# Keys of 14 tiles summed by transfers from GpSimd in place of additions on VectorE, in a linear-attention block with an MLP

## The chip, the cores and the metric

One Trainium2 chip; the kernel uses one core of it. The metric is the device time of one execution in microseconds (us). A core has TensorE (PE, matmuls and, on a track of its own, PEld, the loads of its weights), VectorE (DVE), ScalarE (ACT), GpSimd (POOL) and SyncE (SP), which here only issues transfers (DMAs). Each engine runs its own list of instructions in order; engines wait for one another through semaphores. Transfers are carried out by 16 DMA engines that all issuers share.

## The reference

The input is one sequence of 2048 rows with 512 features. The kernel computes a linear-attention block with 32 heads and then a two-layer MLP, both with a layer norm ahead and a residual behind:

```
h  = x + A(layernorm(x), wqkv, wo)
h2 = h + relu(layernorm(h) @ w1) @ w2            # 512 -> 1792 -> 512

A:  q, k, v = split((x @ wqkv)), 32 heads of 16
    phi(t) = where(t > 0, t + 1, exp(t)) + 1e-6
    pq, pk = phi(q), phi(k)
    kv  = sum over s of pk[s] (outer) v[s]       # per head, 16 x 16
    z   = sum over s of pk[s]                    # per head, 16
    o   = (pq @ kv) / (pq . z + 1e-6)
    A   = o @ wo
```

The change concerns z, the sum of the key features pk over all 2048 rows.

## The kernel before

**Tiling.** The 2048 rows are 16 tiles of 128 rows (`t` = 0 to 15), each tile with its rows on the 128 partitions. Transposed data (features on partitions) is kept in 4 chunks of 512 rows. All intermediate data stays on the chip.

**Order.** There is no automatic scheduling. The string `ORDER` (line 18 on) lists all work as words such as `K.5.1`; the name picks a function `op_...`, the numbers are its arguments. The words are issued in this order, and each engine runs its own part of the list in that order. So a word that waits holds up all later words of the same engine, and no others directly.

**Words around the change**, in the order in which a key tile passes through them:

- `S`, `A` (VectorE): statistics of a tile of x; `R` (ScalarE): 1/sqrt of the variance; `N` (VectorE, line 251): the normalized tile.
- `T` and `E` or `V`: transpose of the normalized tile on TensorE and its copy by ScalarE or VectorE; for most tiles `X` (line 291) instead, a transposing transfer issued by SyncE.
- `K` (TensorE, line 299): the keys of one tile, four matmuls into one PSUM bank.
- `F` (ScalarE, line 317): exp of the keys; `U` (ScalarE, line 320): relu of the keys; `M` (VectorE, line 324): min(exp, 1) + 1e-6; `D` (VectorE, line 327): their sum, pk, in bf16. From tile 4 on these four words handle two tiles at once.
- `G` (TensorE, line 351): adds the tile's part of x-transposed times pk into four banks, from which kv is later made.
- `za` (VectorE, line 358): adds two tiles of pk to `z_acc`, an fp32 array of 128 partitions by 2 x 512, one half for the even tile and one for the odd tile of each pair. It lies in memory that the MLP uses only later. `za.2` adds the pairs (0, 1) and (2, 3); five more words add one pair each, up to tiles 12 and 13.
- `zf` (VectorE, lines 362 to 364): adds the two halves of `z_acc` and splits the fp32 result into two bf16 arrays, value and remainder.
- `z` (TensorE, line 370): column sums over the 128 partitions: for each of the four blocks of 128 features, four matmuls of one column each, over pk of tiles 14 and 15 and the two arrays of `zf`.
- `zc`, `zh` (VectorE): z out of PSUM and, masked by head, as the matrix that the denominators (`dn`, TensorE, line 448) multiply.

Between these stand `Q` (TensorE, line 307), the queries, with `qF`, `qU`, `qM`, `qD` for their features, and words that load weights through SyncE: `lk`, `lq`, `lv`, `lo`, `l1`, `l2`. GpSimd builds masks at the start and has no other work.

`ORDER` has the following stretch on VectorE around the end of the sums (words of other engines left out): `M.10.2 za.8 D.12.2 D.10.2 za.10 za.12 ... M.14.2 ... zf.12 D.14.2 ... qM.0.0.2 qD.0.2.2 zc qD.0.0.2 zh`. On TensorE it is `K.14.2 G.9 K.15.3 G.10 Q.0.3.1 Q.0.2.0 G.11 G.12 z.0.2.14 z.2.2.14 z.1.2.14 z.3.2.14 G.13 G.14 dn.0.0 G.15`.

Of the kernel before, what the change touches and what calls it, by code (L numbers as in the profile page):

```python
# [9 lines left out]
ALU = mybir.AluOpType  # L10
# [6 lines left out]

ORDER = """
const table lx.0.1 lx.2.1 S.0 lx.1.1 S.2 A.0 S.1 A.2 R.0.1 N.0 R.2.1 lx.3.1 lk.0.2 lx.4.2 masks warm.1.7
warm.9.7 A.1 R.1.1 T.0.6 S.3 warm.1.7 N.2 T.2.4 N.1 A.3 E.0 R.3.1 T.1.5 lk.2.2 S.4 E.1 N.3 A.4 V.2 S.5 A.5  # L20
K.0.6 lx.6.2 K.1.3 T.3.1 F.0.1 U.0.1 lx.8.4 E.3 K.2.0 M.0.1 S.6 D.0.1 K.3.2 A.6 S.7 F.1.1 M.1.1 lx.12.4 R.4.2
N.5 A.7 N.4 U.1.1 D.1.1 F.2.1 U.2.1 R.6.2 S.8 S.9 N.7 A.9 A.8 M.2.1 N.6 lq.0.2 G.0 T.5.1 E.5 T.4.3 G.1 X.7
K.5.1 D.2.1 E.4 K.4.0 R.8.2 T.6.3 G.2 N.9 X.9 F.3.1 U.3.1 S.12 N.8 S.13 X.8 lq.2.2 M.3.1 A.13 A.12 D.3.1 E.6
K.6.2 F.4.2 R.12.2 U.4.2 K.7.3 G.3 M.4.2 S.11 F.6.2 U.6.2 N.12 D.4.2 S.10 S.14 N.13 M.6.2 A.11 A.10 D.6.2 A.14
R.10.2 X.12 K.9.1 G.4 N.11 S.15 N.10 A.15 X.13 K.8.0 G.5 G.6 za.2 U.8.2 F.8.2 X.11 X.10 G.7 R.14.2 K.13.1
K.12.0 M.8.2 N.15 D.8.2 za.4 N.14 K.11.3 K.10.2 G.8 l2.0.3 F.12.2 U.12.2 za.6 X.15 X.14 Q.0.0.0 F.10.2 Q.0.1.1
lv.2.2 l1.0.2 M.12.2 lv.0.2 l2.10.4 U.10.2 qU.0.0.2 qF.0.0.2 M.10.2 za.8 D.12.2 D.10.2 za.10 za.12 K.14.2 G.9
K.15.3 F.14.2 U.14.2 G.10 Q.0.3.1 Q.0.2.0 M.14.2 qF.0.2.2 qU.0.2.2 G.11 zf.12 D.14.2 G.12 z.0.2.14 z.2.2.14
z.1.2.14 z.3.2.14 qM.0.2.2 l2.7.3 lo.0.2 lo.2.2 l1.2.2 qM.0.0.2 qD.0.2.2 G.13 zc G.14 qD.0.0.2 zh dn.0.0 G.15
gD.2.2 gD.0.2 Q.1.1.3 Q.1.0.2 dnl.0 dnx.0.0.2 Q.1.2.0 dnx.0.2.2 kv.3.4 kv.0.4 kv.1.4 kv.2.4 Q.1.3.1 qF.1.0.2  # L30
qM.1.0.2 kx qF.1.2.2 qW.1.0.2 dt.0 dt.3 dt.2 dt.1 m.2.6 m.1.5 m.3.7 m.0.4 mA.0.2 Q.2.0.2 Q.2.1.3 qM.1.2.2
mA.2.2 qW.1.2.2 dn.1.5 dm.0.0.2 dm.0.2.2 dnl.1 dnx.1.2.2 Q.2.3.1 h.3.5 hD.3 h.0.6 h.1.7 hD.0 s.3 dnx.1.0.2
dt.6 Q.2.2.0 dt.4 dt.7 dt.5 qF.2.0.2 qU.2.0.2 h.2.6 hD.1 Q.3.0.2 Q.3.1.3 s.0 qF.2.2.2 qU.2.2.2 s.1 qU.3.0.2
a.3 a.0 hD.2 qM.2.0.2 n.0 a.1 n.1 dm.1.0.2 dm.1.2.2 n.3 s.2 Q.3.2.0 Q.3.3.1 qD.2.0.2 a.2 qM.2.2.2 n.2 qF.3.0.2
qF.3.2.2 l2.3.4 x.0 qM.3.2.2 qD.2.2.2 h.5.6 h.7.7 h.6.5 x.1 t.2.3 r.0.4 e.2 h.4.4 x.3 dn.2.3 dnl.2 dnx.2.0.2
p.0.0.2 dt.8 hD.6 qM.3.0.2 qW.3.2.2 hD.4 p.0.1.3 qD.3.0.2 hD.5 dnx.2.2.2 pA.0.0.2 p.0.3.1 p.0.2.0 dn.3.6
pD.0.2.2 p.0.5.3 p.0.4.2 pD.0.4.2 p.0.7.1 p.0.6.0 p.0.13.3 s.6 dt.10 p.0.12.2 dt.11 dt.9 hD.7 a.6 s.5 dm.2.0.2
dm.2.2.2 dnl.3 pA.0.6.2 a.5 pD.0.12.2 f.2.6.0.7 s.7 h.11.7 h.9.0 p.0.9.3 h.8.5 p.0.8.2 dnx.3.2.2 dnx.3.0.2
hD.9 a.7 hD.11 p.0.10.0 f.3.7.0.7 p.0.11.1 h.10.4 dt.15 pA.0.10.2 pD.0.8.2 dt.14 dt.13 dt.12 s.4 s.9 n.5
dm.3.2.2 s.11 hD.8 a.11 dm.3.0.2 hD.10 n.7 f.2.6.7.7 h.13.5 h.15.4 n.6 hD.15 a.4 n.4 s.8 h.14.1 f.3.7.7.7  # L40
h.12.2 f.0.4.0.7 x.5 x.6 s.10 hD.14 a.10 hD.13 hD.12 n.10 x.4 s.13 s.12 x.7 n.11 a.9 a.8 f.1.5.0.7 a.12 s.15
p.1.1.1 p.1.0.0 pA.1.0.2 f.1.5.7.7 a.15 s.14 fo.2 p.1.8.0 p.1.9.1 n.12 a.13 fo.3 n.15 n.13 fo.1 pD.1.8.2
f.0.4.7.7 a.14 n.8 p.1.12.0 p.1.13.1 p.1.2.2 p.1.3.3 p.1.10.6 r.12.4 r.4.4 pA.1.12.2 n.9 x.11 x.15 x.10 x.9
x.8 pD.1.2.2 p.1.7.5 p.1.5.1 fd.2 fd.3 p.1.4.0 p.2.3.3 p.2.2.2 n.14 fo.0 pD.1.4.2 pD.2.2.2 fd.0 x.13 x.14
p.2.0.0 p.1.11.7 p.2.7.3 p.2.1.1 r.8.4 pA.2.0.2 p.2.6.2 p.1.6.4 pD.2.6.2 p.2.4.0 pA.1.10.2 pA.1.6.2 p.2.5.1
pA.2.4.2 f.7.7.0.7 p.2.12.0 p.2.13.1 f.4.4.0.7 f.5.5.0.7 p.2.10.2 f.4.4.7.7 p.2.11.3 f.6.6.0.7 pD.2.10.2
pD.2.12.2 fd.1 x.12 f.6.6.7.7 f.5.5.7.7 p.2.8.0 p.2.9.1 p.3.2.2 p.3.3.3 fo.6 pD.2.8.2 fo.4 fo.5 p.3.4.0
f.7.7.7.7 p.3.5.1 pA.3.4.2 pD.3.2.2 fo.7 f.10.6.0.7 p.3.1.1 f.9.5.0.7 p.3.7.3 p.3.0.0 f.8.4.0.7 p.3.6.2 fd.6
f.9.5.7.7 f.11.7.0.7 f.10.6.7.7 fd.4 fd.5 fd.7 pA.3.0.2 pA.3.6.2 f.8.4.7.7 p.3.12.0 fo.9 f.11.7.7.7 p.3.13.1
p.3.11.3 p.3.10.2 pD.3.10.2 fo.8 fo.11 pA.3.12.2 p.3.9.1 f.13.5.0.7 p.3.8.0 f.12.4.0.7 pA.3.8.2 fo.10 fd.10  # L50
fd.9 f.13.5.7.7 f.14.6.0.7 fo.13 f.12.4.7.7 f.15.5.0.14.3.1 f.14.6.7.7 f.15.7.0.14.0.2 fd.13 fd.8 fd.11 fo.12
fo.14 fo.15.3.1 f.15.4.0.14.2.1 fd.12 fd.14 fd.15.3.1 fo.15.0.2 fo.15.2.1 fd.15.0.2 fd.15.2.1
"""


# [1 line left out]
def kernel(  # L57
# [10 lines left out]
    nc = tc.nc  # L68
# [3 lines left out]
    S, D = xf.shape  # L72
# [70 lines left out]
    z_acc = acts[1][:, 0:4, :].rearrange("p a n -> p (a n)").bitcast(F32).rearrange("p (a n) -> p a n", a=2)  # L143
# [3 lines left out]
    def pk(t, n=1):  # L147
        return pk_lo[:, t : t + n, :] if t < 2 else acts[0][:, t - 2 : t - 2 + n, :]
# [204 lines left out]
                start=(t == 0), stop=(t == NT - 1),  # L353
            )

    def op_za(t):
        first = pk(0, 2) if t == 2 else z_acc
        nc.vector.tensor_tensor(out=z_acc, in0=first, in1=pk(t, 2), op=ALU.add)

    def op_zf(t):  # L360
        z0, z1 = z_acc[:, 0, :], z_acc[:, 1, :]
# [219 lines left out]
```

## Time and profile before

| | |
|---|---|
| median of 3 runs | 170.3 us (169.75 to 170.35) |
| span of the profiled execution, from the first to the last instruction | 168.6 us |
| TensorE busy | 163.1 us, 97% of the span |
| VectorE busy | 104.7 us, 62% |
| ScalarE busy | 64.3 us, 38% |
| GpSimd busy | 4.8 us, 3% |
| share of the 16 DMA engines used by SyncE's queue | 34.6% |

The page gives the span of the profiled execution and no other time of it; the median of the runs is 1.7 us above that span. The page also draws the span in 40 slices of 4.2 us, each digit a busy share in tenths: TensorE stands at 9 from the third slice to the last but one; VectorE stands at 9 or 8 in nearly all slices up to 38 us and falls later; the DMA engines are busiest at 4 to 13 us (x and the first weights) and at 25 to 38 us (all other weights).

How to read the views. A group gives line, engine and operation, then output and inputs (partitions x elements and type), the count, and after the bar the busy time, the mean duration of one in ns, and the idle time of the engine just before. The timeline gives start, duration and the instruction, with the idle time ahead of it and what ended it. A row of transfers gives the KB of each and the median time from issue to landing. The view of the chain that ended last gives start, length, and what the end depended on at that time.

### The profile page before, as it was taken

The numbers are of one execution on the slowest core, as the hardware profiler recorded it, in microseconds if no ns is written. First come the engines' busy times: TensorE is split into PE (matmuls) and PEld (weight loads), VectorE is DVE, ScalarE is ACT, GpSimd is POOL, SyncE is SP. The second block draws the span as 40 slices with busy tenths as digits, with TensorE's granted clock in tenths as the row PEclk, the third lists the DMA queues.
The fourth block names the chain that finished last, engine by engine and source line by source line (L and its number), as shares of the span: only waits on it lengthen the run. The fifth ranks groups of instructions, "written<-read, shape, count | busy, mean of one in ns | idle before, by whom it ended". The sixth has DMA issues, their size and how long they took to land.

```text
span 168.6 us, 2307 instructions
## 1 busy us (share of the span) xinstructions
PE 163.1 (97%) x875; PEld 76.3 (45%) x875; DVE 104.7 (62%) x207; ACT 64.3 (38%) x97; POOL 4.8 (3%) x21
## 2 busy tenths in 40 slices
PE   7799999999999999999999999999999999999993
PEld 2354444444554354444444444444444444444463
DVE  3999999996879896978799725220066401007132
ACT  3699867775589755600201140170000203021000
POOL 7400000000000000000000000000000000000000
PEclk9999999999999999999999999999999999999999
DMA  4972847896414653232142343400000200000232
GB/s 130 295 254 47 146 79 176 312 365 230 95 31 93 156 97 79 45 74 50 41 83 40 62 90 100 91 4 0 0 0 31 93 4 0 0 0 0 79 111 62
DMA packets 30091, 15.36 MB, mean 91 GB/s; under 512 B 22656, under 2 KB 29056, under 8 KB 30080
## 3 DMA queue, kind: packets, MB, share of 16 engines
q1 hardware_dynamic: 30080, 15.21, 34.6%
q8 instruction: 7, 0.11, 0.3%
q14 instruction: 4, 0.03, 0.1%
HBM read 7.86 MB, written 2.10 MB: 59 GB/s over the span
## 4 chain that ended last, share of the span: by engine, by line
PE 84%; ACT 4%; DMA 4%; SPq 3%; DVE 2%; issue 1%; DVEq 0%; ACTq 0%
PE bk L530 29%; PE bk L510 29%; PE bk L351 7%; PE bk L299 7%; PE bk L494 6%; PE bk L307 5%; DMA wk_sb<-in_A_wqkv_dram 3%; ACT eb L317 1%; DMA rd<-wk_sb 1%; SPq L201 1%; SPq L480 1%; PE bk L448 1%; ACT rb L320 1%; DVE pqT L332 1%; ACT lnT L280 1%
## 5 line engine op out<-in xcount | busy, mean ns | idle before, releaser
L530 PE MATMUL bk<-w_sb,at 128*128 128x512 bf16 (+2 forms) x252 | 51.5, 355 | 0.0
L510 PE MATMUL bk<-lnT,w_sb 128*128 128x512 bf16 x224 | 51.4, 379 | 0.0
L516 ACT ACTIVATE at<-bk 128x1024 bf16<-128x1024 f32 x14 | 14.1, 1023 | 70.3 <-PE bk L510 70.3
L521 DVE TENSOR_SCALAR at<-bk 128x1024 bf16<-128x1024 f32 x14 | 17.0, 1221 | 33.7 <-PE bk L510 33.7
L530 PEld LDWEIGHTS <-at 128*128 128x128 bf16 x252 | 23.6, 98 | 25.2
L510 PEld LDWEIGHTS <-w_sb 128*128 128x128 bf16 x224 | 21.8, 98 | 26.0 <-issue 0.2
L538 DVE SCALAR_TENSOR_TENSOR gT<-bk,rstd,h_nat 128x512 bf16<-128x512 f32 (+2 forms) x18 | 12.0, 686 | 18.3 <-PE bk L530 15.9
L317 ACT ACTIVATE eb<-bk 128x1024 bf16<-128x1024 f32 (+1 forms) x18 | 16.5, 925 | 6.1 <-PE bk L299 3.5
L299 PE MATMUL bk<-wk_sb,lnT 128*128 128x512 bf16 x64 | 15.5, 379 | 0.6 <-DMA wk_sb<-in_A_wqkv_dram 0.5
L494 PE MATMUL bk<-m_sb,pqs 128*128 128x512 bf16 x64 | 15.5, 379 | 0.1
L307 PE MATMUL bk<-lnT,wq_sb 128*128 128x512 bf16 x64 | 15.1, 379 | 0.1
L320 ACT ACTIVATE rb<-bk 128x1024 bf16<-128x1024 f32 (+1 forms) x15 | 13.6, 906 | 1.2 <-PE bk L307 1.2
L351 PE MATMUL bk<-at,h_nat 128*128 128x512 bf16 x56 | 13.7, 379 | 0.0
L500 DVE TENSOR_TENSOR h_nat<-bk,x_nat 128x512 bf16<-128x512 f32 x16 | 10.8, 678 | 2.7 <-PE bk L494 2.6
L226 DVE BATCH_NORM_STATS2 st<-x_nat 128x6 f32<-128x512 bf16 x16 | 10.6, 678 | 1.8 <-DMA x_nat<-in_A_x_dram 1.8
L228 DVE BATCH_NORM_STATS2 st<-h_nat 128x6 f32<-128x512 bf16 x16 | 10.5, 679 | 0.0
L299 PEld LDWEIGHTS <-lnT 128*128 128x128 bf16 x64 | 5.9, 98 | 8.2 <-ACT lnT L280 1.2
L494 PEld LDWEIGHTS <-pqs 128*128 128x128 bf16 x64 | 6.1, 98 | 7.9 <-DVE pqs L484 1.2
L307 PEld LDWEIGHTS <-wq_sb 128*128 128x128 bf16 x64 | 6.1, 97 | 7.3 <-issue 0.4
L351 PEld LDWEIGHTS <-h_nat 128*128 128x128 bf16 x64 | 6.0, 98 | 6.6
L461 ACT ACTIVATE wk_sb<-ld 128x1024 bf16<-128x1024 f32 x8 | 8.0, 1048 | 0.1
L324 DVE TENSOR_SCALAR eb<-eb 128x1024 bf16<-128x1024 bf16 (+1 forms) x18 | 6.9, 388 | 1.2 <-ACT eb L317 1.1
(57 smaller groups left out, 90.3 us busy)
## 6 DMA issues: line engine op xcount, KB each, us to landing
out_dram<-gT SPq DMA_DIRECT2D x15, 128.0 KB, 1.8
w_sb<-in_B_w_dram SPq DMA_DIRECT2D x2, 896.0 KB, 6.7
x_nat<-in_A_x_dram SPq DMA_DIRECT2D x2, 512.0 KB, 7.8
w_sb<-in_B_w_dram SPq DMA_DIRECT2D x2, 512.0 KB, 5.2
w_sb<-in_B_w_dram SPq DMA_DIRECT2D x2, 384.0 KB, 5.1
x_nat<-in_A_x_dram SPq DMA_DIRECT2D x4, 128.0 KB, 2.2
wk_sb<-in_A_wqkv_dram SPq DMA_DIRECT2D x2, 256.0 KB, 3.7
x_nat<-in_A_x_dram SPq DMA_DIRECT2D x2, 256.0 KB, 4.1
```

What stands on the lines that cost most here:

```text
L299: nc.tensor.matmul(bk[:, b, :], lhsT=lnT[c][:, kd, j * P : (j + 1) * P], rhs=wk_sb[:, kd, :], start=(kd == 0), stop=(kd == KD - 1),)
L307: nc.tensor.matmul(bk[:, b, :], lhsT=wq_sb[:, kd, j * P : (j + 1) * P], rhs=lnT[c][:, kd, :], start=(kd == 0), stop=(kd == KD - 1),)
L317: nc.scalar.activation(out=buf(eb, kind, i, n), in_=bank(at_bank[kind, i], n), func=ACT.Exp)
L320: nc.scalar.activation(out=buf(rb, kind, i, n), in_=bank(at_bank[kind, i], n), func=ACT.Relu)
L351: nc.tensor.matmul(bk[:, KD + kd, :], lhsT=ln_nat[:, t, kd * P : (kd + 1) * P], rhs=pk(t)[:, 0, :], start=(t == 0), stop=(t == NT - 1),)
L494: nc.tensor.matmul(bk[:, b, :], lhsT=pqs[:, (c * KD + jb) % NQ, j * P : (j + 1) * P], rhs=m_sb[:, jb, :], start=(jb == 0), stop=(jb == KD ...
L500: nc.vector.tensor_tensor(out=h_nat[:, t : t + n, :], in0=bank(at_bank["h", t], n), in1=x_nat[:, t : t + n, :], op=ALU.add,)
L510: nc.tensor.matmul(bk[:, b, cols], lhsT=w1_sb[:, kd, f * P : (f + 1) * P], rhs=lnT[c][:, kd, cols], start=(kd == 0), stop=(kd == KD - 1),)
L516: nc.scalar.activation(out=acts[c % 2][:, f : f + n, :], in_=bank(at_bank["p", c, f], n), func=ACT.Relu)
L521: nc.vector.tensor_scalar(out=acts[c % 2][:, f : f + n, :], in0=bank(at_bank["p", c, f], n), scalar1=0.0, scalar2=None, op0=ALU.max,)
L530: nc.tensor.matmul(bk[:, b, 0 : w * P], lhsT=acts[c % 2][:, f, j * P : (j + 1) * P], rhs=w2_sb[:, f, k * P : (k + w) * P], start=(f == 0), ...
L538: nc.vector.scalar_tensor_tensor(out=o_t[:, t % NO, cols], in0=bk[:, at_bank["f", t, k], 0 : w * P], scalar=rstd2[:, t : t + 1], in1=h_nat ...
```

## The change

The word `za` no longer runs on VectorE. It issues a transfer from GpSimd. The first one, `za.0.1`, copies pk of tiles 0 and 1 into `z_acc` and converts bf16 to fp32; each of the other six (`za.2`, `za.4`, `za.6`, `za.8`, `za.12`, `za.10`) reads a pair of bf16 tiles and adds it to `z_acc` in fp32. `zf`, `z` and all else stay as they are.

```
-    def op_za(t):
-        first = pk(0, 2) if t == 2 else z_acc
-        nc.vector.tensor_tensor(out=z_acc, in0=first, in1=pk(t, 2), op=ALU.add)
+    def op_za(t, first=0):
+        if first:
+            nc.gpsimd.dma_start(out=z_acc, in_=pk(t, 2))
+        else:
+            nc.gpsimd.dma_start(out=z_acc, in_=pk(t, 2), accum_op=ALU.add)
```

In `ORDER` each `za` moves to the place right behind the `D` that completes its pair, and the six words of VectorE are gone from between the others; the words of all other names keep their order. Each stretch below is before, then after:

```
-N.4 U.1.1 D.1.1 F.2.1
+N.4 U.1.1 D.1.1 za.0.1 F.2.1
...
-lq.2.2 M.3.1 A.13 A.12 D.3.1 E.6
+lq.2.2 M.3.1 A.13 A.12 D.3.1 za.2.0 E.6
...
-M.4.2 S.11 F.6.2 U.6.2 N.12 D.4.2 S.10 S.14 N.13 M.6.2 A.11 A.10 D.6.2 A.14
+M.4.2 S.11 F.6.2 U.6.2 N.12 D.4.2 za.4.0 S.10 S.14 N.13 M.6.2 A.11 A.10 D.6.2 za.6.0 A.14
...
-K.8.0 G.5 G.6 za.2 U.8.2 F.8.2
+K.8.0 G.5 G.6 U.8.2 F.8.2
...
-M.8.2 N.15 D.8.2 za.4 N.14 K.11.3 K.10.2 G.8 l2.0.3 F.12.2 U.12.2 za.6 X.15
+M.8.2 N.15 D.8.2 za.8.0 N.14 K.11.3 K.10.2 G.8 l2.0.3 F.12.2 U.12.2 X.15
...
-qF.0.0.2 M.10.2 za.8 D.12.2 D.10.2 za.10 za.12 K.14.2
+qF.0.0.2 M.10.2 D.12.2 za.12.0 D.10.2 za.10.0 K.14.2
```

More of the change, by code (lines that the diff above doesn't have):

```diff
@@ L19 @@
 const table lx.0.1 lx.2.1 S.0 lx.1.1 S.2 A.0 S.1 A.2 R.0.1 N.0 R.2.1 lx.3.1 lk.0.2 lx.4.2 masks warm.1.7
[L20 to L27, printed above, removed]
+warm.9.7 A.1 R.1.1 T.0.6 S.3 warm.1.7 N.2 T.2.4 N.1 A.3 E.0 R.3.1 T.1.5 lk.2.2 S.4 E.1 N.3 A.4 V.2 S.5 A.5 K.0.6
+lx.6.2 K.1.3 T.3.1 F.0.1 U.0.1 lx.8.4 E.3 K.2.0 M.0.1 S.6 D.0.1 K.3.2 A.6 S.7 F.1.1 M.1.1 lx.12.4 R.4.2 N.5 A.7
+N.4 U.1.1 D.1.1 za.0.1 F.2.1 U.2.1 R.6.2 S.8 S.9 N.7 A.9 A.8 M.2.1 N.6 lq.0.2 G.0 T.5.1 E.5 T.4.3 G.1 X.7 K.5.1
+D.2.1 E.4 K.4.0 R.8.2 T.6.3 G.2 N.9 X.9 F.3.1 U.3.1 S.12 N.8 S.13 X.8 lq.2.2 M.3.1 A.13 A.12 D.3.1 za.2.0 E.6
+K.6.2 F.4.2 R.12.2 U.4.2 K.7.3 G.3 M.4.2 S.11 F.6.2 U.6.2 N.12 D.4.2 za.4.0 S.10 S.14 N.13 M.6.2 A.11 A.10 D.6.2
+za.6.0 A.14 R.10.2 X.12 K.9.1 G.4 N.11 S.15 N.10 A.15 X.13 K.8.0 G.5 G.6 U.8.2 F.8.2 X.11 X.10 G.7 R.14.2 K.13.1
+K.12.0 M.8.2 N.15 D.8.2 za.8.0 N.14 K.11.3 K.10.2 G.8 l2.0.3 F.12.2 U.12.2 X.15 X.14 Q.0.0.0 F.10.2 Q.0.1.1
+lv.2.2 l1.0.2 M.12.2 lv.0.2 l2.10.4 U.10.2 qU.0.0.2 qF.0.0.2 M.10.2 D.12.2 za.12.0 D.10.2 za.10.0 K.14.2 G.9
 K.15.3 F.14.2 U.14.2 G.10 Q.0.3.1 Q.0.2.0 M.14.2 qF.0.2.2 qU.0.2.2 G.11 zf.12 D.14.2 G.12 z.0.2.14 z.2.2.14
@@ L30 @@
 gD.2.2 gD.0.2 Q.1.1.3 Q.1.0.2 dnl.0 dnx.0.0.2 Q.1.2.0 dnx.0.2.2 kv.3.4 kv.0.4 kv.1.4 kv.2.4 Q.1.3.1 qF.1.0.2
[L31 to L49, printed above, removed]
@@ L50 @@
-p.3.11.3 p.3.10.2 pD.3.10.2 fo.8 fo.11 pA.3.12.2 p.3.9.1 f.13.5.0.7 p.3.8.0 f.12.4.0.7 pA.3.8.2 fo.10 fd.10
-fd.9 f.13.5.7.7 f.14.6.0.7 fo.13 f.12.4.7.7 f.15.5.0.14.3.1 f.14.6.7.7 f.15.7.0.14.0.2 fd.13 fd.8 fd.11 fo.12
-fo.14 fo.15.3.1 f.15.4.0.14.2.1 fd.12 fd.14 fd.15.3.1 fo.15.0.2 fo.15.2.1 fd.15.0.2 fd.15.2.1
+qM.1.0.2 kx qF.1.2.2 qW.1.0.2 dt.0 dt.3 dt.2 dt.1 m.2.6 m.1.5 m.3.7 m.0.4 mA.0.2 Q.2.0.2 Q.2.1.3 qM.1.2.2 mA.2.2
+qW.1.2.2 dn.1.5 dm.0.0.2 dm.0.2.2 dnl.1 dnx.1.2.2 Q.2.3.1 h.3.5 hD.3 h.0.6 h.1.7 hD.0 s.3 dnx.1.0.2 dt.6 Q.2.2.0
@@ new lines @@
+dt.4 dt.7 dt.5 qF.2.0.2 qU.2.0.2 h.2.6 hD.1 Q.3.0.2 Q.3.1.3 s.0 qF.2.2.2 qU.2.2.2 s.1 qU.3.0.2 a.3 a.0 hD.2
+qM.2.0.2 n.0 a.1 n.1 dm.1.0.2 dm.1.2.2 n.3 s.2 Q.3.2.0 Q.3.3.1 qD.2.0.2 a.2 qM.2.2.2 n.2 qF.3.0.2 qF.3.2.2
+l2.3.4 x.0 qM.3.2.2 qD.2.2.2 h.5.6 h.7.7 h.6.5 x.1 t.2.3 r.0.4 e.2 h.4.4 x.3 dn.2.3 dnl.2 dnx.2.0.2 p.0.0.2 dt.8
+hD.6 qM.3.0.2 qW.3.2.2 hD.4 p.0.1.3 qD.3.0.2 hD.5 dnx.2.2.2 pA.0.0.2 p.0.3.1 p.0.2.0 dn.3.6 pD.0.2.2 p.0.5.3
+p.0.4.2 pD.0.4.2 p.0.7.1 p.0.6.0 p.0.13.3 s.6 dt.10 p.0.12.2 dt.11 dt.9 hD.7 a.6 s.5 dm.2.0.2 dm.2.2.2 dnl.3
@@ new lines @@
+pA.0.6.2 a.5 pD.0.12.2 f.2.6.0.7 s.7 h.11.7 h.9.0 p.0.9.3 h.8.5 p.0.8.2 dnx.3.2.2 dnx.3.0.2 hD.9 a.7 hD.11
+p.0.10.0 f.3.7.0.7 p.0.11.1 h.10.4 dt.15 pA.0.10.2 pD.0.8.2 dt.14 dt.13 dt.12 s.4 s.9 n.5 dm.3.2.2 s.11 hD.8
+a.11 dm.3.0.2 hD.10 n.7 f.2.6.7.7 h.13.5 h.15.4 n.6 hD.15 a.4 n.4 s.8 h.14.1 f.3.7.7.7 h.12.2 f.0.4.0.7 x.5 x.6
+s.10 hD.14 a.10 hD.13 hD.12 n.10 x.4 s.13 s.12 x.7 n.11 a.9 a.8 f.1.5.0.7 a.12 s.15 p.1.1.1 p.1.0.0 pA.1.0.2
+f.1.5.7.7 a.15 s.14 fo.2 p.1.8.0 p.1.9.1 n.12 a.13 fo.3 n.15 n.13 fo.1 pD.1.8.2 f.0.4.7.7 a.14 n.8 p.1.12.0
@@ new lines @@
+p.1.13.1 p.1.2.2 p.1.3.3 p.1.10.6 r.12.4 r.4.4 pA.1.12.2 n.9 x.11 x.15 x.10 x.9 x.8 pD.1.2.2 p.1.7.5 p.1.5.1
+fd.2 fd.3 p.1.4.0 p.2.3.3 p.2.2.2 n.14 fo.0 pD.1.4.2 pD.2.2.2 fd.0 x.13 x.14 p.2.0.0 p.1.11.7 p.2.7.3 p.2.1.1
+r.8.4 pA.2.0.2 p.2.6.2 p.1.6.4 pD.2.6.2 p.2.4.0 pA.1.10.2 pA.1.6.2 p.2.5.1 pA.2.4.2 f.7.7.0.7 p.2.12.0 p.2.13.1
+f.4.4.0.7 f.5.5.0.7 p.2.10.2 f.4.4.7.7 p.2.11.3 f.6.6.0.7 pD.2.10.2 pD.2.12.2 fd.1 x.12 f.6.6.7.7 f.5.5.7.7
+p.2.8.0 p.2.9.1 p.3.2.2 p.3.3.3 fo.6 pD.2.8.2 fo.4 fo.5 p.3.4.0 f.7.7.7.7 p.3.5.1 pA.3.4.2 pD.3.2.2 fo.7
@@ L53 @@
+f.10.6.0.7 p.3.1.1 f.9.5.0.7 p.3.7.3 p.3.0.0 f.8.4.0.7 p.3.6.2 fd.6 f.9.5.7.7 f.11.7.0.7 f.10.6.7.7 fd.4 fd.5
+fd.7 pA.3.0.2 pA.3.6.2 f.8.4.7.7 p.3.12.0 fo.9 f.11.7.7.7 p.3.13.1 p.3.11.3 p.3.10.2 pD.3.10.2 fo.8 fo.11
+pA.3.12.2 p.3.9.1 f.13.5.0.7 p.3.8.0 f.12.4.0.7 pA.3.8.2 fo.10 fd.10 fd.9 f.13.5.7.7 f.14.6.0.7 fo.13 f.12.4.7.7
+f.15.5.0.14.3.1 f.14.6.7.7 f.15.7.0.14.0.2 fd.13 fd.8 fd.11 fo.12 fo.14 fo.15.3.1 f.15.4.0.14.2.1 fd.12 fd.14
+fd.15.3.1 fo.15.0.2 fo.15.2.1 fd.15.0.2 fd.15.2.1
 """
```

## The prediction

> **What bounds the kernel now.** I read the page's busy times first, then the table of busy time by stretch, to see in which stretch TensorE ever lacks work.
>
> ```profile
> span 168.6 us, 2307 instructions
> PE 163.1 (97%) x875; PEld 76.3 (45%) x875; DVE 104.7 (62%) x207; ACT 64.3 (38%) x97; POOL 4.8 (3%) x21
> ```
>
> ```profile
> 13.75:23.40 9.65, 9.65 (x48) 4.44 (x49) 9.65 (x30) 8.40 (x16) 0.00 (x0) 1.00 0.55 98
> 23.40:37.30 13.90, 13.90 (x67) 6.25 (x65) 13.43 (x22) 10.06 (x13) 0.00 (x0) 1.00 0.83 255
> 37.30:57.30 20.00, 19.88 (x145) 9.71 (x144) 15.80 (x30) 14.55 (x17) 0.00 (x0) 1.00 0.47 118
> 57.30:165.90 108.60, 108.53 (x560) 51.02 (x560) 54.80 (x95) 22.16 (x31) 0.00 (x0) 1.00 0.22 51
> ```
>
> The columns are the stretch, its length, then busy time and count of PE, PEld, DVE, ACT and POOL, the granted clock, the DMA share and GB/s. TensorE (PE) and VectorE (DVE) are both full in the first two stretches, but only TensorE stays full to the end: from 13.75 us on it is idle for 0.00 + 0.00 + 0.12 + 0.07 = 0.2 us. A busy TensorE could still be running slowly, so the next view is the chain that ended last:
>
> ```profile
> 24.50 3.45 PE bk L299 x16
> ...
> 35.73 1.73 PE bk L351 x8
> 37.45 0.38 PE bk L370 x16
> ```
>
> Sixteen matmuls of 512 columns in 3.45 us are 0.216 us each, and the eight of L351 keep the same step. TensorE is at its pace here, and VectorE, though full, is not late for it. Taking work off VectorE can therefore win at most the 0.2 us of TensorE's gaps. The question becomes what the new path of the sums costs, and how near it lies to TensorE's order.
>
> **What is removed.** The six additions on VectorE:
>
> ```profile
> L358 DVE TENSOR_TENSOR at<-at,at 128x1024 f32<-128x1024 f32 x5 | 6.1, 1224 | 0.1
> L358 DVE TENSOR_TENSOR at<-pk_lo,at 128x1024 f32<-128x1024 bf16 x1 | 1.2, 1193 | 0.0
> ```
>
> 6.1 + 1.2 = 7.3 us of VectorE, all inside 23.4 to 34.4 us, where TensorE has no gap to close. Gain: 0, with 0.2 us as its upper bound. It does let some key tiles finish sooner, which I use below.
>
> **What is added: a chain of seven transfers.** Each one names the same accumulator, so each must wait until the one before has landed; and each needs its key tiles. When the tiles are ready is read from VectorE's timeline (L327 writes the keys, L362 starts the final reduction zf):
>
> ```profile
> 12.08 0.42 DVE L327 TENSOR_TENSOR pk_lo<-rb,eb 128x512 bf16<-128x512 bf16 x1
> ...
> 17.13 0.42 DVE L327 TENSOR_TENSOR at<-rb,eb 128x512 bf16<-128x512 bf16 x1
> ...
> 29.15 0.43 DVE L324 TENSOR_SCALAR eb<-eb 128x1024 bf16<-128x1024 bf16 x1 [0.34 <-ACT eb L317]
> 29.50 1.22 DVE L358 TENSOR_TENSOR at<-at,at 128x1024 f32<-128x1024 f32 x1
> 30.63 1.29 DVE L327 TENSOR_TENSOR at<-rb,eb 128x1024 bf16<-128x1024 bf16 x2
> ...
> 34.69 0.69 DVE L362 TENSOR_TENSOR at<-at 128x512 f32<-128x512 f32 x1
> ...
> 36.48 0.68 DVE L327 TENSOR_TENSOR at<-rb,eb 128x1024 bf16<-128x1024 bf16 x1
> ```
>
> Tiles 0 and 1 are ready at 12.08 + 0.42 = 12.50 us, tile 3 at 17.55. So the first transfer has 5 us, and the six that add start at 17.55. The last key pairs (12, 13, then 10, 11) end at 31.92; without the addition at 29.50 they follow directly on the L324 row, which waits for ScalarE and can't move. ScalarE's relu of tiles 10, 11 also stands in the way:
>
> ```profile
> 29.00 1.04 ACT L320 ACTIVATE rb<-bk 128x1024 bf16<-128x1024 f32 x1
> ```
>
> It ends at 30.04. Tiles 12 and 13 can then be ready at about 29.5 + 0.65 = 30.2 us, tiles 10 and 11 at 30.8. With L the time from one adding transfer's start to the next one's, the sums are complete at the later of 17.55 + 6L and 30.2 + 2L. They are wanted at 34.69, when zf starts today.
>
> **What is queued behind that wait.** zf sits on VectorE; behind it in order are the key tiles 14 and 15 (36.48), and behind those the column sums on TensorE:
>
> ```profile
> 37.22 0.52 PEld L370 LDWEIGHTS <-at 128*128 128x128 bf16 x16 [0.26 <-DVE at L327]
> 37.29 0.54 PE L370 MATMUL bk<-ones,at 128*128 128x1 bf16 x16
> ```
>
> The weight load waited 0.26 us for exactly that instruction, so there is no slack. TensorE's order is fixed; whatever zf is late, TensorE is idle and the end moves, one for one. The query features of VectorE, the copy of z and the masked z wait in the same queue; they follow as they do now. Nothing queued on GpSimd suffers: its last work before was
>
> ```profile
> 3.45 2.78 POOL L181 TENSOR_SCALAR_AFFINE_SELECT erep<-erep 32x128 bf16<-32x128 bf16 x8
> ```
>
> done at 6.2 us. So loss = max(17.55 + 6L, 30.2 + 2L) - 34.69, if positive. No loss needs L under 2.25 us; up to 3.16 us the loss grows by 2 us for each us of L, beyond by 6.
>
> **L from rows.** No transfer of before goes from GpSimd, none converts, none adds. The nearest rows:
>
> ```profile
> out_dram<-gT SPq DMA_DIRECT2D x15, 128.0 KB, 1.8
> ...
> out_dram<-gT SPq DMA_DIRECT2D x2, 32.0 KB, 1.5
> out_dram<-gT SPq DMA_DIRECT2D x1, 64.0 KB, 1.6
> ```
>
> ```profile
> L201 SPq DMA_DIRECT2D x_nat<-in_A_x_dram x8: 400/430/468, 0.8 to 5.1; - x8
> ```
>
> ```profile
> L291 SPq DMA_TRANSPOSE lnT<-h_nat x9: 1188/1199/1276, 14.0 to 27.4; - x9
> ```
>
> ```profile
> GB/s 325 247 227 212 192 16 0 74 184 184 379 354 289 315 401 430 401 387 416 387 418 303 393 389 365 389 389 377 393 357 356 373 328 348 365 336 340 361 348 358
> DMA packets 3382, 3.18 MB, mean 318 GB/s; under 512 B 1179, under 2 KB 3123, under 8 KB 3382
> ```
>
> - Fixed part: the landings of 32, 64 and 128 KB go back to 1.4 us at no bytes.
> - Issue: 0.43 us for a plain copy, 1.2 us for a transpose, both on SyncE. An issue on GpSimd is neither; I take the middle, 0.8 us.
> - Movement: an adding transfer reads 256 KB of bf16 keys and 512 KB of sums, and writes 512 KB of sums. The engines move some 390 GB/s when they are full (the last view, 28 to 38 us, a slice each 0.25 us). If writing overlaps reading, 786 KB take 2.0 us.
>
> L = 1.4 + 0.8 + 2.0 = 4.2 us, an estimate. From about 30 to 38 us the engines are full of weights:
>
> ```profile
> 29.25 0.46 SPq L204 DMA_DIRECT2D w_sb<-in_B_w_dram  x1
> 29.75 0.48 SPq L204 DMA_DIRECT2D wv_sb<-in_A_wqkv_dram  x1
> 30.27 1.03 SPq L204 DMA_DIRECT2D w_sb<-in_B_w_dram  x2
> 31.34 1.01 SPq L204 DMA_DIRECT2D wo_sb<-in_A_wo_dram  x2
> ```
>
> An adding transfer that shares them moves at half the pace, +2.0 us; two of the six fall there: 6 x 4.2 + 2 x 2.0 = 29.2, complete at 17.55 + 29.2 = 46.75, loss 12.1 us.
>
> Bounds of L: below, 1.4 us and only the 512 KB written at the slice of 430 GB/s, 1.2 us: 2.6 us, complete at 30.2 + 5.2 = 35.4, loss 0.7 us. Above, an issue of 1.2 us and reading and writing in turn, 1,311 KB at the mean of 318 GB/s: 1.4 + 1.2 + 4.1 = 6.7 us, complete at 57.8, loss 23.1 us. I stay between, because reads and writes are two sides of one transfer and the transposes, read and written in SBUF too, land in 2.5 us without a doubled time.
>
> The Trainium skill ("SBUF — State Buffer", section "A bandwidth-pool intuition that's wrong (but worth ruling out)") has a rule against this change: the descriptors of a transfer issued from GpSimd are written by its own cores, which are locked out of a shared port pair while VectorE runs an operation in a two-port mode. By it a bf16 operation such as the L324 row, 0.43 us, could hold up each of the first transfers once; six such waits would make the loss 6 x 0.43 = 2.6 us larger. It fades by itself here, since VectorE stands still once zf waits; my sum leaves it out. The skill's "DMA: Bandwidth & Descriptors" (section "Anatomy of one DMA — SWDGE (gpsimd) path") speaks the other way: about 2.0 us plus the bytes at 436 GB/s, an estimate of 3.2 us for the 512 KB written; six of these would end at 36.75, a loss of 2.1 us. No run so far shows either.
>
> **A cold start on top.** When TensorE starts the kernel, it is slow at first:
>
> ```profile
> 1.25 3.85 PE L215 MATMUL bk<-m_sb 128*128 128x512 bf16 x10 [1.25 <-DVE ones L177]
> ```
>
> Ten matmuls in 3.85 us against ten times 0.216: 1.7 us lost. After some 12 us of idling I expect nearly the same, 1.5 us; bounds 0 and 1.7.
>
> **What may slow the rest.** The new traffic, 256 KB in and 512 KB in and out for each transfer, competes with the transposes of the normalized tiles (row L291 above) and with the weights. A late transpose would make TensorE wait ahead of 37.29; but the sums are then later still, so that wait comes out of the same loss and isn't added. The weights are needed only after the column sums.
>
> **Sum.** 168.6 - 0 + 12.1 + 1.5 = 182.2 us for the span. The page gives the span alone; the median of the runs, 170.3 us, is 1.7 us above it. The same 1.7 us around the new span: 183.9, say 184 us.
>
> **Rivals.**
> - *In time, no loss.* The transfers are short, L up to 2.25 us (2.6 still loses only 0.7 us); zf starts as today, and VectorE's 7.3 us vanish in its own slack: 170.1 to 171.0 us. For it: the 1.5 us of a 32 KB store. Against it: the last two must land one after another between 30.2 and 34.69, while the engines are full, and with 16 times the bytes. It decides at L = 2.25, and it is the one way not to be slower. 8% (with a gain over 0.5% in it 2%, which would need gaps that the trace doesn't have).
> - *Short chain.* L between 2.7 and 3.4 us: losses of 0.9 to 3.3 us, little cold start: 171 to 174 us. For it: 1.4 us and 786 KB at 390 GB/s are 3.4 us, if the issue costs nothing beyond them. Against it: the engines are full while the last two move, and somebody must work out 128 rows of three streams. 13%. The Trainium skill's figure on transfers from GpSimd (the page and section named above) would give a time inside this case.
> - *Long chain.* The converting add moves in turn, or GpSimd writes its descriptors slowly: L of 5.9 us and more, 17.55 + 35.4 + 4.0 = 57.0, loss 22.3 + 1.5: 194 us and up. For it: three streams in one transfer, on a queue that no row prices. Against it: the transposes, with an issue of 1.2 us, still land in 2.5 us. 19%.
> - *My forecast*, L between 3.4 and 5.9 us: 174 to 194 us, 60%.
>
> **How the numbers follow.** 184 us is the forecast. The range is 172 to 197 us: it leaves out the case in time and the slowest part of the long chain, about 2 in 10. A measurement of this kernel can tell about 0.5% from no change, 0.85 us here; a loss under that needs L under 2.7 us. Faster 0.02, same 0.08, slower 0.90.
>
> **What would show it.** VectorE's L362 (moved by two lines) idle ahead for some 12 us, released by a DMA of GpSimd's queue; TensorE idle for the same time before the column sums, full before and after; matmuls behind the gap slower for a few us; transfers on a new queue, each starting only after the last has landed, 4 to 6 us apart. The forecast is wrong if zf starts by 35.5, if TensorE's gap is elsewhere (a late transpose or weight), or if the transfers don't follow one another.

## The result and the profile after

The changed kernel takes 194.07 us (median of 3 runs, 193.14 to 194.57) against 170.3 us: a ratio of 1.140, 95% interval 1.1345 to 1.1457. The profiled execution spans 192.8 us, 24.2 us more than before. Its page:

```profile
span 192.8 us, 2320 instructions
PE 165.5 (86%) x875; PEld 76.5 (40%) x875; DVE 98.1 (51%) x201; ACT 64.3 (33%) x97; POOL 10.8 (6%) x28
...
PE   7899977930005999999999999999999999999994
...
PEclk9999999995555999999999999999999999999999
```

VectorE's busy time fell by 6.6 us. TensorE has a hole of some four slices of 4.8 us, and its clock is at half for about as long. TensorE's timeline shows where the hole lies:

```profile
25.41 3.63 PE L299 MATMUL bk<-wk_sb,lnT 128*128 128x512 bf16 x16 [1.04 <-DMA lnT<-h_nat]
...
32.98 1.04 PE L299 MATMUL bk<-wk_sb,lnT 128*128 128x512 bf16 x4 [1.35 <-DMA lnT<-h_nat]
...
59.91 0.58 PE L372 MATMUL bk<-ones,at 128*128 128x1 bf16 x16 [19.85 <-DVE at L327]
60.36 3.36 PE L351 MATMUL bk<-at,h_nat 128*128 128x512 bf16 x8
...
64.82 2.75 PE L307 MATMUL bk<-lnT,wq_sb 128*128 128x512 bf16 x12
```

The column sums (L372, L370 before) start at 59.91 us in place of 37.29: 22.6 us late. From there to the query matmuls it takes 64.82 - 59.91 = 4.9 us; before it was 40.68 - 37.29 = 3.4, so 1.5 us are lost again. The same rows before:

```profile
37.69 1.89 PE L351 MATMUL bk<-at,h_nat 128*128 128x512 bf16 x8
...
40.68 2.75 PE L307 MATMUL bk<-lnT,wq_sb 128*128 128x512 bf16 x12
```

22.6 + 1.5 = 24.1 of the 24.2 us. VectorE's timeline names the cause:

```profile
36.84 0.43 DVE L324 TENSOR_SCALAR eb<-eb 128x1024 bf16<-128x1024 bf16 x1 [4.97 <-ACT eb L317]
57.37 0.69 DVE L364 TENSOR_TENSOR at<-at 128x512 f32<-128x512 f32 x1 [20.11 <-DMA at<-at]
```

zf (L364, L362 before) waited 20.1 us for the last adding transfer and started 57.37 - 34.69 = 22.7 us late. On GpSimd's timeline each transfer (L358 copies, L360 adds) stands with the duration of its issue and the idle time ahead of it:

```profile
12.68 0.70 POOL L358 DMA_DIRECT2D at<-pk_lo  x1 [6.44 <-DVE pk_lo L327]
17.74 1.03 POOL L360 DMA_DIRECT2D at<-at  x1 [4.37 <-DVE at L327]
24.93 0.87 POOL L360 DMA_DIRECT2D at<-at  x1 [6.16 <-DVE h_nat L251]
31.28 0.85 POOL L360 DMA_DIRECT2D at<-at  x1 [5.48 <-DVE at L327]
40.66 0.85 POOL L360 DMA_DIRECT2D at<-at  x1 [8.52 <-DMA at<-at]
49.27 0.85 POOL L360 DMA_DIRECT2D at<-at  x1 [7.76 <-DMA at<-at]
53.59 0.85 POOL L360 DMA_DIRECT2D at<-at  x1 [3.47 <-DMA at<-at]
```

From one add to the next, and from the last to zf, it takes 7.2, 6.4, 9.4, 8.6, 4.3 and 3.8 us: 39.6 us from 17.74 to 57.37. (Where the row names VectorE as releaser at 24.93 and 31.28, that instruction lies close by chance: the keys had been written by 19.35 and 21.99 us.) The view of transfers gives the landings of all adds together, the copy's, and those of the weights and transposes beside them:

```profile
at<-at POOLq DMA_DIRECT2D x6, 512.0 KB, 6.2
...
at<-pk_lo POOLq DMA_DIRECT2D x1, 512.0 KB, 3.1
...
wo_sb<-in_A_wo_dram SPq DMA_DIRECT2D x2, 256.0 KB, 9.0
...
lnT<-h_nat SPq DMA_TRANSPOSE x9, 3.2
```

Before, wo landed after 6.8 us and the transposes after 2.5: the traffic slows both sides. From 45 to 60 us, in slices of 0.375 us, the engines look like this:

```profile
DMA  9999999810000009999900000059999700000000
```

The long block at the left is the last of the weights with an add among them. The two short blocks are the last two adds alone: some 2 us of movement each, in 4.3 and 3.8 us. The rest is issue, the way to the first byte, landing, and GpSimd's wait.

The same view also counts packets by queue (q0 is GpSimd's, q1 SyncE's; packets, MB, share of the engines' time), and so shows where a slow add spends its time. For the add issued at 40.66 us, from 40.66 to 44.9 and from 44.9 to 49.27 us:

```profile
q1 hardware_dynamic: 1276, 1.58, 109.3%
```

```profile
q0 software_dynamic: 144, 0.52, 46.6%
q1 hardware_dynamic: 141, 0.45, 27.7%
```

In the first 4.3 us only SyncE's queue moves; the add has no packet yet, though VectorE stands still. Then it moves, with the larger share. The first packets of the four slow adds come 2.4, 1.7, 5.2 and 4.3 us after the issue, those of the last two after 1.3 and 1.4 us. From the first packet to the landing it takes 4.3, 4.1, 3.6 and 3.8 us, against 2.4 to 2.5. Of the 14 us that the four lose against the last two, 8 lie ahead of the first packet and 6 behind it.

### The profile page after: what moved, and what is told of

The parts are those of the page before. It is cut to its first block, busy times and chain, and to the rows that moved or that the text cites. A ratio compares the mean times of both kernels' runs of the same rounds, so it can differ in the third digit from the quotient of the medians.

```text
span 192.8 us, 2320 instructions
## 1 busy us (share of the span) xinstructions
PE 165.5 (86%) x875; PEld 76.5 (40%) x875; DVE 98.1 (51%) x201; ACT 64.3 (33%) x97; POOL 10.8 (6%) x28
## 4 chain that ended last, share of the span: by engine, by line
PE 63%; DMA 18%; DVE 9%; ACT 3%; issue 3%; SPq 2%; POOLq 0%; DVEq 0%; ACTq 0%
PE bk L532 25%; PE bk L512 25%; DMA at<-at 13%; PE bk L496 6%; PE bk L307 2%; DMA wk_sb<-in_A_wqkv_dram 2%; DVE st L226 2%; DMA lnT<-h_nat 2%; PE bk L351 2%; ACT eb L317 2%; DVE at L327 1%; PE bk L299 1%; DMA rd<-wk_sb 1%; SPq L201 1%; DVE h_nat L251 1%
## 5 line engine op out<-in xcount | busy, mean ns | idle before, releaser
L372 PE MATMUL bk<-ones,at 128*128 128x1 bf16 x16 | 0.6, 166 | 19.9 <-DVE at L327 19.9
L351 PE MATMUL bk<-at,h_nat 128*128 128x512 bf16 x56 | 15.2, 411 | 0.0
L226 DVE BATCH_NORM_STATS2 st<-x_nat 128x6 f32<-128x512 bf16 x16 | 10.6, 677 | 1.8 <-DMA x_nat<-in_A_x_dram 1.8
L364 DVE TENSOR_TENSOR at<-at 128x512 f32<-128x512 f32 x1 | 0.7, 693 | 20.1 <-DMA at<-at 20.1
L456 ACT ACTIVATE ld<-bk,eps 128x128 f32<-128x128 f32 x4 | 1.5, 368 | 25.5 <-PE bk L450 25.5
```

The source lines that it names most:

```text
L226: op_S = lambda t: nc.vector.bn_stats(out=st[:, t, :], in_=x_nat[:, t, :])
L351: nc.tensor.matmul(bk[:, KD + kd, :], lhsT=ln_nat[:, t, kd * P : (kd + 1) * P], rhs=pk(t)[:, 0, :], start=(t == 0), stop=(t == NT - 1),)
```

## The experiments

The theory: TensorE pays for the lateness of zf one for one. That lateness is the chain of waits for landings, and while weights and transposes are in the engines each link takes about twice its own time. The rivals: VectorE's relief counts too; the adds are slow in themselves, or VectorE holds GpSimd up; bytes, not waits, set the chain. In kernels whose `ORDER` is written in fewer or more lines, line numbers differ by a few.

**VectorE's relief alone.** Five of the six additions are left out and nothing takes their place; z lacks tiles 4 to 13.

```
-za.4 za.6 za.8 za.10 za.12          (words of ORDER; za.2 stays)
```

> The kernel before with five of its six additions left out and nothing in their place; z then lacks tiles 4 to 13. Theory: TensorE sets the end and has 0.2 us of gaps after 13.75 us, so taking 6.1 us off VectorE moves the time by 0 to -0.3 us: 170.0 to 170.4 us. Rival: VectorE, full up to 38 us, also sets the end, and freeing it is worth 1 us or more: 169.3 us or less.

Measured: 170.26 us, ratio 0.9992 (0.9968 to 1.0015). The stretch that was full on both engines:

```profile
23.40:37.30 13.90, 13.90 (x80) 6.48 (x79) 7.95 (x17) 9.96 (x12) 0.00 (x0) 1.00 0.90 260
```

VectorE is busy for 7.95 us of it, in place of 13.43; TensorE still for all 13.90. The relief is worth nothing that can be measured.

**Without the large weights beside it.** The loads of w1 and w2 are moved behind the column sums, in the changed kernel and in the kernel before.

```
-l2.0.3 ... l1.0.2 ... l2.10.4 ... l2.7.3 ... l1.2.2     (among the adds)
+... dt.1 l1.0.2 l1.2.2 ... x.3 l2.0.3 l2.10.4 l2.7.3    (behind the sums)
```

> The changed kernel with the loads of w1 and w2 moved behind the column sums. In the changed kernel the adding transfers take 6.4 to 9.4 us from issue to issue while the engines carry weights, and 4.3 us at the end, when they are alone. Theory: the weights ahead in the engines make the difference; without them the chain from 31.28 us on takes about 5.5 + 3 x 4.3 us, zf starts at 49 to 50.5 us in place of 57.4, and the time falls by 7 to 8 us, to 186 to 187 us, if the moved weights are not late themselves (the next run shows that). Rival: each adding transfer is slow by itself in that stretch (VectorE holds up GpSimd, or the add is slow): zf stays at 56 to 58 us, 193 to 195 us.

> The kernel before with the same loads moved in the same way: what the move costs by itself. Both theories: 170.3 us, or up to 2 us more if a weight or a transpose behind it is late; the run before it is read against this one.

Measured: the changed kernel 187.57 us, ratio to the kernel before 1.099 (1.092 to 1.107); the kernel before with the same move 170.77 us, ratio 1.0024 (1.0001 to 1.0047). The move costs 0.5 us by itself and takes 6.5 us off the changed kernel. GpSimd's timeline of the first:

```profile
18.31 1.02 POOL L358 DMA_DIRECT2D at<-at  x1 [4.37 <-DVE at L325]
25.86 0.87 POOL L358 DMA_DIRECT2D at<-at  x1 [6.52 <-DVE at L325]
30.62 1.08 POOL L358 DMA_DIRECT2D at<-at  x1 [3.89 <-DMA at<-at]
37.33 0.85 POOL L358 DMA_DIRECT2D at<-at  x1 [5.63 <-DMA at<-at]
41.60 0.85 POOL L358 DMA_DIRECT2D at<-at  x1 [3.42 <-DMA at<-at]
45.94 0.85 POOL L358 DMA_DIRECT2D at<-at  x1 [3.48 <-DMA at<-at]
```

The fourth step shrank from 8.6 to 4.3 us and zf started at 49.8 us, as the theory had it. The time missed the theory's 186 to 187 us: zf came 7.6 us sooner, but TensorE's slow start grew from 1.5 to 2.5 us (58.24 - 52.30 = 5.9 us from the column sums to the query matmuls, against 3.4), and the move itself costs 0.5. The first step stays at 7.5 us: there the transposes and the query weights are in the engines, which this run leaves where they were and no run took away; the third, 6.7 us, still has the loads of wv and wo beside it.

**Keeping TensorE busy while it waits.** 85 matmuls on zeros stand ahead of the column sums.

```
-... G.12 z.0.2.14 ...
+... G.12 warm.85.2 z.0.2.14 ...
```

> The changed kernel with 85 matmuls on zeros, 18.3 us of them, put into TensorE's idle time ahead of the column sums. Theory: the eight matmuls behind the gap took 3.2 us in place of 1.7 because the granted clock had fallen to half during the wait; kept busy, TensorE starts at full pace: 1.5 us less, 192.4 to 192.8 us, and zf as late as it was (57 to 58 us). Rival: the slow start has another cause (a wait for VectorE or the late query features): 194 us as the changed kernel, or more.

Measured: 194.32 us, ratio 1.1385 (1.1337 to 1.1432): no gain. TensorE's timeline:

```profile
40.08 18.51 PE L213 MATMUL bk<-m_sb 128*128 128x512 bf16 x85
60.10 0.55 PE L370 MATMUL bk<-ones,at 128*128 128x1 bf16 x16 [1.51 <-DVE at L325]
60.51 1.89 PE L349 MATMUL bk<-at,h_nat 128*128 128x512 bf16 x8
...
73.27 2.93 PE L494 MATMUL bk<-m_sb,pqs 128*128 128x512 bf16 x12 [0.93 <-DVE pqs L484]
```

The mechanism was right, the time was not: it is the one that the rival gave, though not by the rival's cause. The eight matmuls behind the wait take 1.89 us in place of 3.36, and no slow start is left. But 0.9 us of it is given back at 73.27, where VectorE was late because one transposing transfer of the denominators took 4.26 us on the chain that ended last; in the changed kernel the transfer on that chain took 2.43 us. Why it was slow here wasn't tried, so what the slow start costs in the end stays open between about 0 and 1.5 us.

**Transfers that don't add.** All seven are converting copies; each overwrites the one before, so z holds only tiles 10, 11, 14 and 15.

```
-            nc.gpsimd.dma_start(out=z_acc, in_=pk(t, 2), accum_op=ALU.add)
+            nc.gpsimd.dma_start(out=z_acc, in_=pk(t, 2))
```

> The changed kernel with all seven transfers as converting copies, none of which adds; each overwrites the one before, so z holds only tiles 10, 11, 14 and 15. In the changed kernel the one copy moves for 1.4 us and lands 3.1 us after its issue, an add that is alone moves for 2.0 us and lands after 3.8 us. Theory: adding costs 0.7 us of the 4.3, the rest is the issue, the way to the first byte, the landing and the wait behind weights; zf starts at 51 to 54 us in place of 57.4: 188 to 191 us. Rival: the add itself makes the transfers long; as copies they take under 3 us and zf starts by 46 us: 183 us or less.

Measured: 185.57 us, ratio 1.090 (1.083 to 1.096), between the two: adding costs more than the theory gave it, and still less than half of the loss. GpSimd's timeline, the last two, and then VectorE's:

```profile
39.65 0.53 POOL L360 DMA_DIRECT2D at<-at  x1 [7.32 <-DMA at<-at]
45.48 0.53 POOL L360 DMA_DIRECT2D at<-at  x1 [5.30 <-DMA at<-at]
```

```profile
48.29 0.69 DVE L364 TENSOR_TENSOR at<-at 128x512 f32<-128x512 f32 x1 [12.15 <-DMA at<-at]
```

zf started at 48.29 us. The last copy, alone, is done in 48.29 - 45.48 = 2.8 us; the last add took 3.8. So an add costs 1.0 us more than a copy when alone, not 0.7: 0.3 of it is the issue, 0.53 against 0.85 us. The six steps take 30.1 us in place of 39.6; the 3.5 us beyond 6 x 1.0 were not taken apart.

**One add alone.** Only the first copy and the last add, tiles 10 and 11; z lacks tiles 2 to 9, 12 and 13.

```
-za.2.0 za.4.0 za.6.0 za.8.0 za.12.0       (words of ORDER; za.0.1 and za.10.0 stay)
```

> The changed kernel with the first copy and the last add (tiles 10 and 11) alone; z lacks tiles 2 to 9, 12 and 13. Theory: the weights ahead in the engines hold up even a single add, which goes out at about 31 us: as the one at 31.28 us in the changed kernel it lands after 7 to 9 us; zf starts at 38 to 40.5 us in place of 34.7: 174 to 177 us. Rival: only the length of the chain costs; a lone add lands after 3.8 us, zf starts at 34.8 us: 170 to 171 us.

Measured: 177.69 us, ratio 1.044 (1.035 to 1.052), 0.7 us above the theory's range of times. GpSimd's timeline, then VectorE's, then TensorE's:

```profile
31.04 0.88 POOL L358 DMA_DIRECT2D at<-at  x1 [17.43 <-DVE at L325]
```

```profile
40.04 0.69 DVE L362 TENSOR_TENSOR at<-at 128x512 f32<-128x512 f32 x1 [5.44 <-DMA at<-at]
```

```profile
42.58 0.59 PE L370 MATMUL bk<-ones,at 128*128 128x1 bf16 x16 [5.18 <-DVE at L325]
43.03 3.57 PE L349 MATMUL bk<-at,h_nat 128*128 128x512 bf16 x8
```

A single add, with no chain behind it, took 9.0 us from issue to zf, as the one at 31.28 us in the changed kernel (9.4), against 3.8 us alone; its first packet came 5.3 us after the issue. So the wait beside the weights is there without the chain. zf is as late as the theory gave it; what the theory left out is the slow start, which is as long behind 5.2 us of idling (3.57 us for the eight matmuls) as behind 20 (3.36).

**Halves.** Each transfer is cut in two, the even tile and the odd tile, which makes two chains of half the bytes each.

```
+        for i in range(2):
...
+                nc.gpsimd.dma_start(out=z_acc[:, i, :], in_=pk(t + i)[:, 0, :], accum_op=ALU.add)
```

> The changed kernel with every transfer cut in two (even tile, odd tile), which makes two independent chains of half the bytes, 14 issues in all. Theory: of 4.3 us from add to add 2.0 are bytes and 2.3 are fixed; a half takes 3.3 us and the two chains overlap: 1 us less for each of the last two steps, 0 to 1 us for the contended four: zf at 52 to 56 us, 188.5 to 192.5 us. Rival: GpSimd's issues (0.85 us each) or the bytes set the step: 194 us or more.

Measured: 188.0 us, ratio 1.104 (1.098 to 1.111); zf started at 51.32 us:

```profile
51.32 0.69 DVE L365 TENSOR_TENSOR at<-at 128x512 f32<-128x512 f32 x1 [13.66 <-DMA at<-at]
```

A little more came off than the theory gave (6 us of chain in place of 1 to 5). The same bytes with twice the issues are done sooner, so neither the bytes nor GpSimd's issues set the chain by themselves.

**Two sums.** The transfers feed two sums in different memory in turn, and VectorE joins them. The first transfer into each sum is a copy, so there are two copies and five adds.

```
+        acc = z_two if t in (2, 6, 12) else z_acc
...
+        nc.vector.tensor_tensor(out=z_acc, in0=z_acc, in1=z_two, op=ALU.add)
```

> The changed kernel with two sums in different memory, which the transfers feed in turn, and one addition of VectorE (1.2 us) that joins them ahead of zf. Each transfer then waits for the one before the last. Theory: the wait for landing makes the chain, not the engines' pace; with two in flight it ends at about 41 us and zf starts at 41 to 44 us: 176 to 181 us. Rival: the engines' pace makes the chain; two in flight share it, and zf stays above 52 us: 188 us or more.

Measured: 184.05 us, ratio 1.080 (1.072 to 1.088), between the two. VectorE joined the sums at 45.39 us and zf started at 46.65, 10.7 us sooner than in the changed kernel, but not at 41 to 44. GpSimd's and TensorE's timelines show what the expectation left out:

```profile
25.95 0.86 POOL L360 DMA_DIRECT2D at<-at  x1 [2.04 <-DVE h_nat L250]
35.59 1.75 POOL L360 DMA_DIRECT2D at<-at  x2 [8.78 <-DVE at L326]
```

```profile
30.19 2.98 PE L298 MATMUL bk<-wk_sb,lnT 128*128 128x512 bf16 x8 [2.33 <-DMA lnT<-h_nat]
```

With two adds in flight the transposes land later (4.8 us in place of 3.2), TensorE waits 2.3 us for one of them and runs slowly behind it (8 matmuls in 2.98 us), and the last keys come later too: GpSimd waited for them until 35.59 us.

**The traffic alone.** The kernel before, with the copy and the first add (tiles 0 to 3) on GpSimd; VectorE adds the other five pairs.

```
+        if t > 2:
+            nc.vector.tensor_tensor(out=z_acc, in0=z_acc, in1=pk(t, 2), op=ALU.add)
...
+ za.0.1 behind D.1.1 and za.2.0 behind D.3.1; za.4 to za.12 where they were
```

> The kernel before with the first copy and the first add alone on GpSimd (tiles 0 to 3); VectorE adds the other five pairs as before. The add is long done when VectorE needs it. Theory: no chain decides, so what is left is the traffic: in the changed kernel TensorE waited 1.0 us at 25.4 us for a transposed tile behind the first add; that wait, hidden there in the larger one, shows now: 170.8 to 171.8 us. Rival: the transposes have room for it, or VectorE's saved 1.2 us make good: 170.0 to 170.5 us.

Measured: 171.59 us, ratio 1.0084 (1.0056 to 1.0112). TensorE's timeline:

```profile
25.11 3.63 PE L297 MATMUL bk<-wk_sb,lnT 128*128 128x512 bf16 x16 [1.19 <-DMA lnT<-h_nat]
```

The add lands 6.6 us after its issue at 17.46, and VectorE's next addition, at 24.77, does not wait for it; still the kernel is 0.8% slower. TensorE waits 1.2 us for a transposed tile, a wait that the trace of before doesn't have. No kernel here beats the one before. Whatever VectorE is relieved of, TensorE's 0.2 us of gaps from 13.75 us on remain all there is to win.

## Why the prediction was right, and by how much it fell short

The direction and the place came out as forecast, and the path from the chain of landings through zf to TensorE. 194.07 us lies in the range of 172 to 197 us, but that is in part luck: the range reaches into the case of the long chain. From add to add and on to zf it took 39.6 / 6 = 6.6 us on average, which is that case's L (5.9 us and more, 19%) and not the L of the favoured case (3.4 to 5.9 us, 60%); the time stands just past the favoured case's border of 194 us. Point by point:

- *The relief is worth 0.* Right, shown by the run without the sums.
- *One for one.* Right: zf 22.7 us late, the column sums 22.6 us late.
- *When the adds can start.* Right: 17.55 us forecast, 17.74 found, and the first copy was over by then.
- *An add that is alone: 4.2 us.* Right in the sum, 4.3 and 3.8 us found at the end. Its parts: the issue is 0.85 us (0.8 forecast), the movement about 2 us.
- *Two contended adds at +2.0 us each.* This is the term that was mis-sized. Four adds were contended, not two, and they took 7.2 + 6.4 + 9.4 + 8.6 = 31.5 us where the sum had 4 x 4.2 + 4.0 = 20.8. That is 10.7 us; the last two, 8.1 in place of 8.4, give 0.3 back and the start costs 0.2: 10.6, the whole difference between 12.1 and 22.7. I counted only the weights from 30 to 38 us as contention. The prediction's own table had the engines at a share of 0.55 from 13.75 us and 0.83 from 23.4 us on, which is where the first two adds run, beside transposes and query weights. And with the adds among them the weights last until 48 us, in place of 40, into the later adds. The picture behind the 2.0 us was wrong too: not a movement at half the pace (that would give 6.2 us, and the single add took 9.0), but above all a wait of up to 5.2 us for the first packet while SyncE's queue moves. Without w1 and w2 the third add waited 2.7 us for its first packet in place of 5.2, and the fourth 1.4 in place of 4.3, so the loads ahead of it make that wait; why a transfer from GpSimd waits for them so long was not tried.
- *A slow start, 1.5 us.* 1.5 us as found behind the wait, but 2.5 with the late weights, above the bound of 1.7; the run with busy matmuls removed it there, and kept little of it at the end.
- *Late transposes hide in the larger loss.* Right for this kernel, where TensorE waits 1.0 and 1.4 us for them ahead of its hole ("full before" was not so); with a short chain they cost 1.3 us by themselves (the last run). In the run with two sums they made the keys late and with them the sums, a loop that the prediction didn't have.
- *The rivals.* "In time" and "short chain" fell with the landings. "Long chain" gave about the time (194 us and up), and its L, but its cause, slow descriptors or movement in turn in every add, did not come true: alone an add takes 3.8 to 4.3 us.
- *The border of 174 us.* It leaves out the 4.0 us of contention that the upper border holds. With them an L of 3.4 us gives a loss of 17.55 + 6 x 3.4 + 4.0 - 34.69 = 7.3 us, and with the slow start about 179 us.

That VectorE holds up the descriptors of GpSimd's transfers was a rule of the Trainium skill ("SBUF — State Buffer", section "A bandwidth-pool intuition that's wrong (but worth ruling out)"). Of it this trace shows little: the copy at 12.68 us, issued while VectorE worked without a gap, landed after 3.1 us; the adds are issued in 1.03 and 0.87 us while VectorE works, and in 0.85 us at 40.66, 49.27 and 53.59, while it stands still. That is 0.18 us at most, not 0.43 each; and the slow adds at 31.28 and 40.66 us went out with VectorE mostly or wholly idle. The Trainium skill's estimate of 3.2 us for such a transfer ("DMA: Bandwidth & Descriptors", section "Anatomy of one DMA — SWDGE (gpsimd) path") agrees with the copies alone, 2.8 to 3.1 us, but not with the adds, 3.8 us alone and more among other traffic.

## What to carry to other kernels

Read which engine has no gaps before moving work off another: relief of an engine that is full, but not late, is worth nothing. A serial chain of transfers costs its full latency per link, and the price to use is the one among the traffic of that stretch, including the traffic that the chain itself pushes later. Ask what is already queued when a transfer is issued, and not only what share of the engines it will have: here the wait for the first packet cost more than the slower movement. Where such a chain ends in a wait, look at what stands behind that wait in the order of the engine, and at who waits for that.

## What the runs showed of the hardware that was not expected

A converting transfer of 512 KB issued from GpSimd lands 2.8 to 3.1 us after its issue, an adding one after 3.8 us when alone and up to 9.0 us among other transfers, of which up to 5.3 us pass before its first packet. SyncE's own issue suffers as well; in the changed kernel one plain load of wo was issued in 3.42 us, where both took some 0.5 us before:

```profile
L204 SPq DMA_DIRECT2D wo_sb<-in_A_wo_dram x2: 562/1992/3422, 33.5 to 37.0; - x2
```

TensorE's granted clock follows its idling within a few us. By stretches of the changed kernel (the clock is the third number from the end):

```profile
40.00:43.00 3.00, 0.06 (x1) 0.00 (x0) 0.00 (x0) 0.31 (x1) 0.85 (x1) 0.98 1.10 368
43.00:44.00 1.00, 0.00 (x0) 0.00 (x0) 0.00 (x0) 0.00 (x0) 0.00 (x0) 0.50 1.12 365
...
62.00:63.00 1.00, 1.00 (x4) 0.43 (x3) 0.00 (x0) 0.00 (x0) 0.00 (x0) 0.50 0.00 0
63.00:64.00 1.00, 1.00 (x20) 0.61 (x19) 0.00 (x0) 0.00 (x0) 0.00 (x0) 0.82 0.00 0
```

Idle from 40.06 us, it is at half by 43 us; at work again from 59.91, it is at full pace between 63 and 64 us. A shorter wait costs no less: behind 5.2 us of idling, in the run with one add, the first eight matmuls took 3.57 us, behind 19.9 us 3.36.
